# A new hand-written order of steps, six weight staging tiles and one PSUM pool in a fused RWKV and squared-ReLU kernel

## Chip, cores and metric

The kernel runs on one core of a Trainium2 chip. The metric is device time in microseconds (us); the kernel before takes 173.77 us (median of 3 runs, 173.72 to 174.05). One core has five engines with queues of their own: TensorE (PE, with its weight loads PEld), VectorE (DVE), ScalarE (ACT), GpSimd (POOL) and SyncE (SP, which here only issues DMAs). A wait on one engine holds all that stands behind it in that engine's queue.

## What is computed

```python
# attention: B, H, S, D = 4, 8, 768, 48
for t in range(S):
    cur = einsum('bhd,bhe->bhde', u * k[t], v[t])
    y[t] = einsum('bhd,bhde->bhe', r[t], state + cur)
    state = w * state + einsum('bhd,bhe->bhde', k[t], v[t])
# feed-forward: x = y as 3072 tokens of 384; w_in 384 x 2048, w_out 2048 x 384
h = maximum(x @ w_in, 0)
out = (h * h) @ w_out
```

All inputs and the output are float32; the kernel computes its matmuls in bfloat16.

## The kernel before

The sequence is cut into 24 chunks of 128 tokens: chunk i is part i // 4 of batch i % 4. Each chunk goes through the same steps, and each step is a method of the class `Do`. `ld` loads r, k or v of a chunk (192 KB each, on SP). `rh` and `kh` scale r and k by powers of w (L339, L336) into a bfloat16 tile `rk`; `T` transposes that tile with eight matmuls on the identity into a PSUM bank (L363) and `Tc` copies it to SBUF, or `XB` does the same by a transposing DMA (L369). `A` makes the two 128 x 512 products of k and r (L376), and `Bm` masks each half on DVE (L384). `Y` multiplies that by v and, from chunk 4 on, adds the part of the carried state (L392, L394). `P0`, `P1`, `du` and `dv` make the term with u, `xs` adds it to Y (L411). `vb` is v in bfloat16. `U` is this chunk's share of the state (L403); `S0`, `ts` and `S` carry the state on. `X` and `xTc`, or `xX` as a DMA, transpose xs into xT (L429, L436).

The feed-forward works on groups: two of one chunk, then eleven of two (`GROUPS`). `F1.g.s` is a slice s of 512 columns of x @ w_in for group g (L445): twelve matmuls for a group of one chunk, six for a pair. `re` takes the ReLU out of PSUM on ACT or DVE (L453, L455), `sq` squares it (L460, L462, L464) into one of 30 `hq` tiles. `F2.i.q` adds a quarter of the second product for chunk i, four matmuls (L472); `os` copies the sum and `out` stores it. `F2c` is F2 for the last chunk in two column parts (L486). `Z.n.b` is filling: n // 4 matmuls of 512 columns and n % 4 of 128 on the identity, whose result nobody reads (L498, L500).

The first weight goes in eight pieces `W1` of 384 KB in float32: seven by `lW` on SP into a staging tile (four tiles, `wsa`) with a cast `cW`, one (W.0.2) by a DMA that casts, issued by POOL. The second weight goes in four pieces `W2` (W.1.0 to W.1.3) by such DMAs from POOL (L333).

Nothing schedules at run time. The text `ORDER` lists all steps; each engine's queue holds its own in that order, and semaphores make a step wait for what it reads and for the tile that it overwrites. A step reads `what:engine/slots`:

```python
for step in ORDER.split():
    what, how = step.split(":")
    name, *at = what.split(".")
    eng, *given = how.split("/")
```

`F1.2.4:P/0` is slice 4 of group 2 on TensorE into slot 0 of its pool. PSUM has eight banks in three pools: four for the attention steps, two for F1 (`bankH`), two for F2 (`bankO`). F2's four quarters of a chunk come in the order 0 to 3.

Of the kernel before, what the change touches and what calls it, by code (L numbers as in the profile page):

```python
# [40 lines left out]
xTc.4:A P1.7:D XB.7:S/6 F2.2.3:P kh.9:D/2 P0.9:D/3 T.6:P/3 rh.9:D F1.3.4:P/0 ld.k.10:S/2 F2.3.3:P Tc.6:A/0 P0.6:D/2
ld.k.8:S/3 vb.6:A/7 re.3.4:A/0 F1.3.3:P/1 A.6:P/2/1 re.3.3:A/4 ld.r.8:S/1 P1.6:G ld.v.8:S/1 os.3:D/2 A.7:P/0/3
F1.3.1:P/0 du.7:D/1 F1.3.5:P/1 S.5:G Bm.6.0:D/3 kh.8:G/1 U.7:P/2 Bm.6.1:D/1 ld.v.10:S/2 re.3.1:A/3 du.6:D/2 re.3.5:A/2
dv.6:G Bm.7.1:D/2 U.4:P/1 Bm.7.0:D/0 sq.3.3:A0/16 F1.3.0:P/0 F1.3.2:P/1 re.3.0:A/5 sq.3.1:A0/17 Y.6:P/3 dv.7:G Y.7:P/0
ld.v.9:S/3 F1.3.7:P/0 ts.4:D/1 XB.9:S/1 out.3:S re.3.2:A/1 xs.6:D/1 sq.3.0:A0/18 vb.8:A/2 U.6:P/1 os.2:D/3 rh.8:G
kh.10:G/0 X.6:P/3 XB.8:S/3 sq.3.2:A0/19 ld.k.11:S/4 F1.3.6:P/1 F2.5.0:P/1 ld.r.10:S/3 F2.4.0:P/0 xs.7:D/2 X.7:P/0
F2.4.1:P xTc.6:A/2 ld.r.11:S/4 F2.5.1:P ts.7:D/0 re.3.6:A/4 re.3.7:D/3 xTc.7:A F1.4.4:P/1 P0.8:G/4 kh.11:G/6 F1.4.6:P/0
S.4:D ld.r.12:S/5 ld.k.13:S/5 sq.3.7:A0/20 ts.6:D/1 P1.8:D sq.3.4:A0/21 du.8:D/3 ld.r.13:S/6 sq.3.5:A0/22 S.7:D
re.4.4:A/5 A.9:P/3/2 sq.3.6:A0/23 dv.8:G ld.v.11:S/5 re.4.6:A/1 A.8:P/0/1 P1.9:D Bm.8.1:D/4 F1.4.1:P/1 rh.10:G P0.11:G/0
F2.4.2:P Bm.8.0:D/5 XB.10:S/2 vb.9:A/1 F1.4.2:P/0 re.4.1:A/3 Bm.9.0:D/3 Y.8:P/1 Bm.9.1:D/1 U.8:P/0 du.9:D/4 ld.k.14:S/6  # L50
F1.4.3:P/1 P1.11:G xs.8:D/3 sq.4.1:A0/24 re.4.2:A/0 sq.4.2:A0/25 F1.4.0:P/0 dv.9:G sq.4.4:A0/26 U.9:P/3 re.4.0:A/2
rh.11:D F2.4.3:P re.4.3:A/4 sq.4.0:A0/27 os.4:A/2 Y.9:P/2 F1.4.7:P/0 X.8:P/1 XB.11:S/4 sq.4.3:A0/28 xs.9:D/4 F1.4.5:P/1
xTc.8:A/0 ts.8:D/0 F2.6.0:P/0 ld.k.15:S/1 X.9:P/2 P0.13:D/1 rh.13:G/4 F2.5.2:P re.4.7:D/3 P0.10:D/2 re.4.5:A/0 xTc.9:A
ld.r.15:S/0 S.6:D vb.10:A/3 sq.4.7:A0/29 F2.6.1:P S.8:G F1.5.7:P/0 out.4:S F1.5.5:P/1 re.5.7:A/5 F2.5.3:P du.11:D/0
F1.5.1:P/0 ts.9:D/1 P1.10:G A.11:P/1/0 Bm.11.0:D/0 sq.4.5:A0/1 vb.11:A/0 A.10:P/2/3 re.5.5:A/2 F1.5.0:P/1 kh.13:G
sq.5.5:A0/0 F2.6.2:P Bm.11.1:D/2 re.5.1:A/4 Bm.10.1:D/5 F1.5.4:P/0 os.5:A/2 U.11:P/1 du.10:D/2 re.5.0:A/3 U.10:P/0
# [61 lines left out]
def kernel(  # L118
# [443 lines left out]
```

## Time and profile before

| what | value |
|---|---|
| device time, median of 3 runs (lowest to highest) | 173.77 us (173.72 to 174.05) |
| span of the profiled execution, first to last instruction | 172.5 us |
| median time minus that span | 1.27 us |
| busy time of PE, DVE, ACT, POOL | 161.6, 130.3, 111.1, 80.8 us |
| DMA | 29.13 MB, mean 169 GB/s |

The profile of one execution numbers every time from the start of its span. "[1.41 <-DVE rk L336]" behind an instruction is the idle time of its engine before it and what ended it. In a row of the timeline stand start, length, engine, line, operation and tiles (written <- read), merged to a count; a matmul's modelled end includes the pipeline, so that rows overlap. In the view by stretches each engine has its busy time and, in brackets, its instructions; at the end stand the granted TensorE clock, the share of DMA time and GB/s. In the chain of waits each row is a piece of the path that ended last: start, length, and what it was.

### The profile page before, as it was taken

To read this page: it belongs to the slowest core of one execution; us is meant where nothing else is said; L and a number is where in the kernel's file an instruction comes from. 1 tells how busy PE (TensorE), PEld (TensorE's weight loads), DVE (VectorE), ACT (ScalarE), POOL (GpSimd) and SP (SyncE) were. 2 spreads that over 40 slices of the span, in tenths; PEclk is the share of its full clock that TensorE was granted. 3 is DMA by queue.
4 is the path that set the end of the run, shared out by engine and by line. 5 is a ranking of instruction groups with operands and counts; after the bars stand their busy time and mean duration, and the time that the engine had idled before them with its cause. 6 is when DMAs were issued, how large, how long until landed. Compare 5 with 4: busy or idle time off the path is not lost.

```text
span 172.5 us, 4388 instructions
## 1 busy us (share of the span) xinstructions
PE 161.6 (94%) x1702; PEld 121.2 (70%) x1702; DVE 130.3 (76%) x259; ACT 111.1 (64%) x207; POOL 80.8 (47%) x98
## 2 busy tenths in 40 slices
PE   3976799979999999999999999999999999999992
PEld 1444788745788787787778768777778778777671
DVE  5768977739999896598789889888889894538300
ACT  2358787746379899858649647848858726532430
POOL 5644895108659298966937364047660204000000
PEclk9999999999999999999999999999999999999999
DMA  5999899989999989979999997998988330331022
GB/s 99 223 244 306 227 188 207 195 166 200 204 212 184 202 177 214 241 174 184 204 189 215 177 229 153 180 181 186 154 217 159 85 114 4 87 141 48 23 78 84
DMA packets 105588, 29.13 MB, mean 169 GB/s; under 512 B 98008, under 2 KB 105568, under 8 KB 105568
## 3 DMA queue, kind: packets, MB, share of 16 engines
q1 hardware_dynamic: 103672, 26.95, 72.7%
q0 software_dynamic: 1744, 1.77, 6.1%
q8 instruction: 13, 0.21, 0.5%
q10 hardware_dynamic: 152, 0.14, 0.2%
q14 instruction: 7, 0.06, 0.1%
HBM read 20.46 MB, written 4.72 MB: 146 GB/s over the span
## 4 chain that ended last, share of the span: by engine, by line
PE 76%; DMA 12%; SPq 8%; ACT 1%; POOL 1%; issue 1%; DVE 0%; POOLq 0%
PE bank L472 33%; PE bank L445 31%; DMA ldk<-in_k_dram 8%; SPq L320 6%; DMA wsa<-in_moe_w_in_dram 4%; PE bank L376 3%; PE bank L394 2%; PE bank L392 2%; SPq L324 2%; PE bank L403 2%; PE bank L486 2%; PE bank L429 1%; PE bank L363 1%; ACT W L260 1%; POOL urow L218 0%
## 5 line engine op out<-in xcount | busy, mean ns | idle before, releaser
L445 PE MATMUL bank<-xT,W 128*128 128x256 bf16 (+1 forms) x624 | 74.9, 264 | 0.2
L472 PE MATMUL bank<-W,hq 128*128 128x384 bf16 x368 | 69.3, 326 | 0.0
L453 ACT ACTIVATE hr<-bank 128x512 bf16<-128x512 f32 x75 | 44.4, 596 | 32.6 <-PE bank L445 27.1
L445 PEld LDWEIGHTS <-W 128*128 128x128 bf16 x624 | 55.2, 98 | 10.6 <-DVE hr L455 0.3
L472 PEld LDWEIGHTS <-hq 128*128 128x128 bf16 x368 | 34.8, 98 | 17.6
L460 ACT ACTIVATE hq<-hr 128x512 bf16<-128x512 bf16 x65 | 39.1, 628 | 0.3
L384 DVE TENSOR_TENSOR Bm<-bank,maskJT 128x512 bf16<-128x512 f32 x48 | 31.3, 684 | 7.3 <-PE bank L376 7.2
L346 POOL TENSOR_TENSOR P<-P,ub 128x384 f32<-128x384 f32 x15 | 16.1, 1079 | 13.9 <-DVE P L342 13.6
L455 DVE TENSOR_SCALAR hr<-bank 128x512 bf16<-128x512 f32 x21 | 14.3, 687 | 8.5 <-ACT hq L460 3.8
L342 POOL TENSOR_TENSOR P<-ldr,ldk 128x384 f32<-128x384 f32 x14 | 14.3, 1022 | 9.6 <-DMA ldk<-in_k_dram 6.0
L336 POOL TENSOR_TENSOR rk<-ldk,Wkhat 128x384 bf16<-128x384 f32 x10 | 10.0, 996 | 16.9 <-DMA ldk<-in_k_dram 16.9
L411 DVE TENSOR_TENSOR xs<-bank,dv 128x384 bf16<-128x384 f32 x24 | 13.0, 552 | 5.0 <-POOL dv L354 2.8
L354 POOL TENSOR_TENSOR dv<-ldv,du 128x384 f32<-128x384 f32 x18 | 14.8, 829 | 0.0
L349 DVE TENSOR_REDUCE du<-P 128x8 f32<-128x384 f32 x24 | 13.0, 544 | 0.6 <-POOL P L346 0.4
L260 ACT COPY rkT<-bank 128x1024 bf16<-128x1024 bf16 x7 | 7.1, 1012 | 9.1 <-PE bank L363 9.1
L339 POOL TENSOR_TENSOR rk<-ldr,Wt 128x384 bf16<-128x384 f32 x9 | 9.0, 996 | 7.0 <-DMA ldr<-in_r_dram 7.0
L260 ACT CAST vb<-ldv 128x384 bf16<-128x384 f32 x19 | 9.6, 511 | 4.1 <-DMA ldv<-in_v_dram 4.1
L498 PE MATMUL bank<-identity 128*128 128x512 bf16 x29 | 9.5, 471 | 2.7 <-POOL identity masks.py:199 2.7
L260 ACT COPY os<-bank 128x384 f32<-128x384 f32 (+1 forms) x15 | 7.0, 469 | 6.8 <-PE bank L472 4.5
L262 DVE COPY os<-bank 128x384 f32<-128x384 f32 (+1 forms) x10 | 5.2, 524 | 7.9 <-PE bank L486 4.3
L394 PE MATMUL bank<-vb,Bm 128*128 128x48 bf16 x192 | 11.0, 183 | 0.0
L464 DVE TENSOR_TENSOR hq<-hr 128x512 bf16<-128x512 bf16 x27 | 10.9, 432 | 0.0
(66 smaller groups left out, 166.5 us busy)
## 6 DMA issues: line engine op xcount, KB each, us to landing
ldk<-in_k_dram SPq DMA_DIRECT2D x24, 192.0 KB, 3.6
ldr<-in_r_dram SPq DMA_DIRECT2D x24, 192.0 KB, 3.6
ldv<-in_v_dram SPq DMA_DIRECT2D x24, 192.0 KB, 4.0
out_dram<-os SPq DMA_DIRECT2D x23, 192.0 KB, 2.3
wsa<-in_moe_w_in_dram SPq DMA_DIRECT2D x7, 384.0 KB, 5.6
W<-in_moe_w_out_dram POOLq DMA_DIRECT2D x4, 384.0 KB, 9.9
rkT<-rk SPq DMA_TRANSPOSE x17, 3.5
W<-in_moe_w_in_dram POOLq DMA_DIRECT2D x1, 192.0 KB, 6.3
```

The lines of the kernel that those rows point to most:

```text
L260: e.copy(o, a)
L342: e.tensor_mul(P0b[slot[f"P{i}"]], loaded("r", i), loaded("k", i))
L346: e.tensor_mul(t, t, ub)
L349: e.tensor_reduce(dub[slot[f"dv{i}"]], P0b[slot[f"P{i}"]], axis=mybir.AxisListType.X, op=ALU.add)
L354: e.tensor_mul(dvb[slot[f"dv{i}"]], loaded("v", i), t)
L384: e.tensor_mul(Bmb[slot[f"Bm{i}{h}"]], heads(bank(f"bA{i}{h}"), 128), mask_b)
L394: e.matmul(y[:, hc, D * h : D * (h + 1)], m[h][:, hc, :], vb[:, 2 * hc + h, :], start=(c == 0), stop=True, skip_group_check=True,)
L445: e.matmul(hp[:, fi, :], W1[f // 2][:, c, 128 * (f % 2) : 128 * (f % 2 + 1)], xt[:, c, :], start=(c == 0), stop=(c == CCH - 1), skip_group ...
L453: e.activation(hr, hp, AF.Relu)
L455: e.tensor_scalar_max(hr, hp, 0.0)
L460: e.activation(hq, hr, AF.Square)
L472: e.matmul(bank(f"bO{i}", "bO")[:, 0:d_model], hqb[slot[f"hq{g},{f // m}"]][:, at : at + L], W2[q][:, f % 4, :], start=(f == 0), stop=(f = ...
```

## The change

The whole of `ORDER` is new. The steps are the same ones, apart from Z; their order on every engine, the engine of some of them and their slots are drawn anew by a model that plays the engines in time order. Counted by engine: on DVE re 21 to 31, xTc 0 to 6, vb 1 to 4, cW 0 to 1, S 10 to 5, kh 14 to 10, P0 10 to 8, P1 9 to 6, os 10 to 8, sq 31 to 25; on ACT re 75 to 65, sq 65 to 71, vb 19 to 9, xTc 14 to 8, os 15 to 17; on POOL S 6 to 11, kh 10 to 14, P0 14 to 16, P1 15 to 18, vb 4 to 11, cW 3 to 2. Z goes from 17 steps (29 matmuls of 512 columns, 7 of 128) to 6 (38 and 14).

The four staging tiles become six (`st`), and the three PSUM pools one of eight banks, where any step can have any bank. F2 names its first f-block and a count, so that the quarters of a chunk may come in any order:

```diff
-POOLS = dict(ldr=7, ldk=7, ldv=7, ws=0, wsa=4, rk=7, P0=5, dv=5, vb=8, rkT=7, bank=4, bankH=2, bankO=2, Bm=6, xs=5, xT1=2, xT2=3, xT4=1, hr=6, hq=30, os=4, ts=2)
+POOLS = dict(ldr=7, ldk=7, ldv=7, st=6, rk=7, P0=5, dv=5, vb=8, rkT=7, Bm=6, xs=5, hr=6, hq=30, os=4, ts=2, xT1=2, xT2=3)
...
-    def bank(var, kind="b"):
-        return banks[first[kind] + slot[var]]
+    def bank(var):
+        return banks[slot[var]]
...
-        def F2(e, i, q):
+        def F2(e, i, f0, nf):
...
-            for f in range(4 * q, 4 * q + 4):
+            for f in range(f0, f0 + nf):
                 at = L * n * (f % m) + L * j
+                summed[i] += 1
                 e.matmul(
-                    bank(f"bO{i}", "bO")[:, 0:d_model],
+                    bank(f"bO{i}")[:, 0:d_model],
                     hqb[slot[f"hq{g},{f // m}"]][:, at : at + L],
-                    W2[q][:, f % 4, :],
-                    start=(f == 0), stop=(f == FCH - 1), skip_group_check=True,
+                    W2[f // 4][:, f % 4, :],
+                    start=(summed[i] == 1), stop=(summed[i] == FCH), skip_group_check=True,
```

The other edits add forms that this version does not use (`PAIRED = 0`, `WIDE = False`, `WCP = False`) and rename tiles (`Wk` to `WkQ`). So the queues begin as follows. SP before, then after:

```
ld.k.1 ld.r.1 u ld.r.3 ld.r.0 ld.k.0 ld.v.1 ld.k.3 ld.r.2 ld.v.0 ld.k.2 lW.0.1 lW.0.6 ld.v.2 lW.0.7 lW.0.0 ld.v.3 lW.0.5 lW.0.4 wc lW.0.3 ld.r.4 ld.k.4 ld.r.5 ld.k.5 ld.k.7 ld.v.5 ld.v.4 ld.r.7 ld.r.6 ld.k.6 ld.v.7
ld.r.0 ld.k.3 u ld.k.0 ld.r.3 ld.r.1 ld.r.2 ld.k.2 ld.k.1 lW.0.0 ld.v.0 lW.0.1 ld.v.3 ld.v.1 ld.v.2 lW.0.4 lW.0.5 lW.0.6 lW.0.7 lW.0.3 ld.r.4 wc ld.k.4 ld.r.5 ld.k.5 ld.r.7 ld.k.7 ld.v.4 ld.v.5 ld.k.6 ld.r.6 ld.v.7
```

TensorE after (slots left out; F2.i.f.4 is four f-blocks from f):

```
Z.83 T.3 T.0 Z.31 A.0 A.3 T.1 Z.22 A.1 T.2 U.0 Y.0 Z.15 X.0 A.2 Z.8 Y.3 Y.1 U.3 F1.0.0 X.3 U.2 X.1 Y.2 F1.1.0 Z.7 F1.0.2 F1.1.2 F1.1.3 X.2 F1.0.3 F1.2.4 F1.2.1 F1.2.3 F1.2.7 F1.2.5 F1.1.1 U.1 F1.2.0 F1.2.6 F1.2.2 F1.0.1 F2.1.0.4 F2.2.0.4 F2.3.0.4 F2.0.0.4 T.4 F2.2.4.4 F2.3.4.4 T.5 F2.0.4.4 F2.1.8.4 A.5 A.4 F2.1.4.4 F2.2.8.4 F2.2.12.4 F2.0.8.4 F2.0.12.4 U.4 Y.4 F2.3.12.4 Y.5 F2.1.12.4 X.4 U.5 X.5 F2.3.8.4 T.6 F1.3.3
```

TensorE before, from the first F1 on:

```
F1.1.3 Y.2 X.0 F1.1.0 F1.0.0 Y.3 X.2 U.0 F1.0.3 X.3 U.3 F1.0.2 F1.1.2 F1.2.1 F1.2.4 F1.2.5 U.1 F1.2.7 F1.0.1 F1.1.1 F1.2.3 F2.0.0 F1.2.2 F2.1.0 F1.2.6 F1.2.0 F2.1.1 F2.0.1 T.4 F2.0.2 F2.1.2 A.4 T.5 F2.0.3 F2.1.3 A.5 F2.3.0 F2.2.0 F2.2.1 Y.4 U.5 Y.5 F2.2.2 F2.3.1 X.4 X.5 F2.3.2 F2.2.3 T.6 F1.3.4 F2.3.3
```

POOL after: `P0.0 P0.3 P1.3 P1.0 P0.1 P1.1 vb.0 dv.0 vb.3 dv.3 dv.1 vb.2 P0.2 P1.2 cW.0.5 W.0.2 cW.0.3 W.1.0 W.1.1 WLm kh.4 P1.4 W.1.2 W.1.3 rh.7 kh.7`. ACT after, from the first copy: `Tc.3 Tc.0 Tc.1 cW.0.0 cW.0.1 Tc.2 vb.1 xTc.0 xTc.3 cW.0.4`. DVE after, from xTc.1: `xTc.1 re.0.0 du.2 dv.2 cW.0.7 xs.2 xTc.2 re.0.2 sq.0.2 sq.1.3 rh.4 re.2.1 sq.2.1 P0.4 sq.1.2 S0.2 S0.1`.

More of the change, by code (lines that the diff above doesn't have):

```diff
@@ L52 @@
[L52 to L56, printed above, removed]
@@ L240 @@
+    nc.gpsimd.memset(maskP if PAIRED else maskJT, 1.0)
+    if PAIRED:
+        for p in rows:
+            above(nc.gpsimd, maskP[p, :], L // 2 + 1)
+    else:
+        above(nc.gpsimd, maskJT, L)
     mask_b = bass.AP(
@@ L371, in A @@
         def A(e, i):
+            if i < PAIRED:
+                tk, tr = [rkTb[slot[f"rkT{x}P{i // 2}"]].rearrange("q (j c) t -> q j c t", j=2) for x in "kr"]
+                for hc in range(HP):
+                    for h in range(2):
+                        q = slice(64 * h, 64 * h + D)
+                        for p in rows:
+                            e.matmul(
+                                heads(bank(f"bA{i}{h}"), 128)[p, hc, :].rearrange("p (j t) -> p j t", j=2),
+                                tk[q, i % 2, hc, p],
+                                tr[q, :, hc, p],
+                                start=True, stop=True, skip_group_check=True,
+                            )
+                return
             t = rkTb[slot[f"rkT{i}"]]
```

463 lines of the change are left out of this document (301 added, 162 removed).

## The prediction

> **What bounds the kernel now.** I read the page first, then the busy times by stretch, then the chain of waits in order of time, then the timeline of the first 48 us.
>
> ```profile
> span 172.5 us, 4388 instructions
> ...
> PE 161.6 (94%) x1702; PEld 121.2 (70%) x1702; DVE 130.3 (76%) x259; ACT 111.1 (64%) x207; POOL 80.8 (47%) x98
> ...
> PE   3976799979999999999999999999999999999992
> ...
> DMA  5999899989999989979999997998988330331022
> ```
>
> ```profile
> 25.00:48.00 23.00, 21.44 (x225) 15.79 (x223) 17.91 (x36) 13.85 (x26) 10.31 (x13) 1.00 1.08 195
> 48.00:160.00 112.00, 112.00 (x1186) 86.20 (x1184) 92.43 (x176) 78.09 (x151) 54.38 (x57) 1.00 0.78 165
> ```
>
> The second row (PE is the first busy figure) decides the frame: from 48 to 160 us TensorE is never idle, so there only its amount of work counts. Between 25 and 48 us it is idle for 23.00 - 21.44 = 1.56 us. Before 25 us much of its time goes to Z, the filling matmuls on the identity. The DMA digits are 9 for the first two thirds.
>
> ```profile
> 24.58 13.90 DMA ldk<-in_k_dram
> 38.50 0.57 DVE rk L336
> 39.12 0.62 PE bank L363 x8
> ...
> 166.68 2.65 PE bank L486 x32
> 169.33 0.02 issue
> 169.35 0.37 ACT os L260
> ```
>
> The one long wait of the dense part: the load k5 lands 13.9 us after its issue, kh.5 follows, and T.5 starts only at 39.12. At the end nothing but F2c, one copy and its store are left: 172.5 - 169.33 = 3.2 us, and the new order ends the same way, with the last copy on DVE instead of ACT.
>
> All times below are of this execution, span 172.5 us. The median of the runs, 173.77, lies 1.27 us above the span; I add 1.27 at the end.
>
> **The change part by part.** Counted from the two orders, TensorE does the same work but for Z: 96 F1, 92 F2, 2 F2c, 24 A, 24 Y, 20 U, 14 X and 7 T in both; Z goes from 29 wide and 7 narrow matmuls to 38 and 14. So three things count: how late the dense work starts, what waits stand in it, and whether the new order brings waits after 48 us.
>
> *Start, to 25.4 us.*
>
> ```profile
> 2.70 5.18 PE L498 MATMUL bank<-identity 128*128 128x512 bf16 x13 [2.70 <-POOL identity masks.py:199]
> ...
> 3.53 0.15 PEld L498 LDWEIGHTS <-identity 128*128 128x128 bf16 x1 [0.28 <-issue]
> 3.96 0.15 PEld L498 LDWEIGHTS <-identity 128*128 128x128 bf16 x1 [0.28 <-issue]
> ...
> 8.91 1.01 ACT L260 COPY rkT<-bank 128x1024 bf16<-128x1024 bf16 x1 [2.89 <-PE bank L363]
> ...
> 14.49 1.28 DVE L384 TENSOR_TENSOR Bm<-bank,maskJT 128x512 bf16<-128x512 f32 x2
> ...
> 15.09 1.24 PE L498 MATMUL bank<-identity 128*128 128x512 bf16 x5
> ...
> 16.75 0.56 DVE L411 TENSOR_TENSOR xs<-bank,dv 128x384 bf16<-128x384 f32 x1 [0.52 <-ACT rkT L260]
> ...
> 17.05 0.89 ACT L260 CAST W<-wsa 128x768 bf16<-128x768 f32 x1
> ...
> 17.85 0.48 ACT L260 COPY xT<-bank 128x384 bf16<-128x384 bf16 x1
> ...
> 20.59 1.56 PE L445 MATMUL bank<-xT,W 128*128 128x128 bf16 x24
> ...
> 25.66 1.21 PEld L445 LDWEIGHTS <-W 128*128 128x128 bf16 x12 [0.29 <-DVE hr L455]
> ```
>
> A wide Z first takes 0.43 us (3.53 to 3.96), later (1.24 - 0.17 of pipeline) / 5 = 0.21; 13 in 5.18 us means ten slow ones. Z.83 (20 wide, 3 narrow) thus lasts 4.3 + 2.1 + 0.2 = 6.6 us, to 9.3, though T.3's inputs are there at about 7.4. T.3 and T.0 follow, their copies Tc.3 and Tc.0 (1.01, spaced 0.92) end at 12.0 with Z.31 beside them, and A.0 starts at 12.0 (before: 11.45). Two Bm (0.60 apart) end at 13.75; T.1, Z.22, A.1, T.2 and U.0 keep TensorE until 15.2; then Y.0, xs.0 (0.56, with Z.15 beside it), X.0 at 16.3, and on ACT Tc.2, vb.1, xTc.0 until 17.6. A.2, Z.8, Y.3, Y.1 and U.3 stand ahead of F1.0.0, which starts at 18.3. F1.1.0, F1.0.2 and F1.1.2 follow (0.76 each) behind X.3, X.1, Y.2 and two casts (0.89), to 22.85.
>
> ```profile
> 7.75 1.00 POOL L342 TENSOR_TENSOR P<-ldr,ldk 128x384 f32<-128x384 f32 x1 [0.72 <-DMA ldk<-in_k_dram]
> ...
> 9.42 1.00 POOL L342 TENSOR_TENSOR P<-ldr,ldk 128x384 f32<-128x384 f32 x1 [0.67 <-DMA ldk<-in_k_dram]
> ...
> 19.17 0.90 ACT L260 CAST W<-wsa 128x768 bf16<-128x768 f32 x1 [0.84 <-DMA wsa<-in_moe_w_in_dram]
> ```
>
> Next comes the data. The fifth load of 192 KB is there at 7.7, the seventh at 9.4; twelve units of 192 KB later (a W1 piece is two) the piece W1.0 is there at 19.15: 0.81 us a unit. In the new SP order W1.7 ends the 24th unit: 7.7 + 19 x 0.81 = 23.1, its cast on DVE (no such row; between 0.6 and 0.9, I take 0.65) ends at 23.75, and F1.1.3 waits 0.9 us for it. The six staging tiles remove SP's waits for a cast; since DMA is full all the same, the bytes come no sooner, and I cost them at nothing (at best the 0.9). F1.1.3, X.2 and F1.0.3 end at 25.4. The old order has done exactly this set when it starts F1.2.1 at 25.66. So this stretch is worth 0.25 us; bounds: -1.0 (W1.7 a us later) to +1.0 (W1.7 on time).
>
> *25.4 us to the point where groups 0 to 2 are through F2 and T.6 is done.*
>
> ```profile
> 47.56 0.82 PE L445 MATMUL bank<-xT,W 128*128 128x256 bf16 x6
> 48.21 0.81 PE L472 MATMUL bank<-W,hq 128*128 128x384 bf16 x4
> ```
>
> F1 is spaced 0.65 and F2 likewise; the smaller ones come from their spacing in the chain. The rest of this set is 8 F1 of group 2 (5.2), two short F1 (1.5), 16 F2 (10.4), three T (1.35), two each of A, Y, U, X (2.0) and U.1: 20.6 us. Before, it ends at 47.56 + one F2 + one U = 48.4, so 22.7 us with 2.1 of waits, T.5's 1.6 the largest. The new order puts T.5 behind as much useful work (21.0 us against 21.2), but the loads r5 and k5 now have fewer weight loads beside them: W.1.2 and W.1.3 stand on POOL behind kh.4, which needs k4.
>
> ```profile
> 24.23 2.18 POOL L333 DMA_DIRECT2D W<-in_moe_w_out_dram  x3
> ```
>
> ```profile
> W<-in_moe_w_out_dram POOLq DMA_DIRECT2D x4, 384.0 KB, 9.9
> ```
>
> The first row issues W.1.1 to W.1.3; the second is the page's, with the median from issue to landing last. In the 13.9 us from k5's issue to its landing, DMA moved nearly all four W2 pieces and four loads of 0.81: at most (13.9 - 3.2) / 4 = 2.7 us for a piece; I take 2.4, since the end of W.0.2 is in it. By the same bytes in the new order, with two pieces still to come and a little of them under way, k5 lands at about 34.8 (an estimate). kh.5 ends at 35.5 to 36.5, T.5 is due at 36.7: no wait. Instead W.1.2 and W.1.3, issued at about 31 and 32, are due at 37.8 (F2.1.8) and 40.2 (F2.2.12). I put their landing at 37 and 39, so no wait, with little cover. On DVE rh.4 and P0.4 wait for r4 and k4 with re.2.1 and S0.2 behind them, whose banks F1.1.1 (28.7) and F1.2.2 (30.9) need: a cover of some 0.4 us. ACT's Tc.5 before A.5 is even (38.35 against 38.45). TensorE then reaches the point at 46.0 to 46.1: 2.3 us sooner than before.
>
> *After it.* The same work at the same spacing; a gain or a loss can only be new waits. Lead of the data: A stands about 2 us of TensorE work later in the new order for most chunks, SP's loads are in nearly the same order, so the lead after the 2.3 us is about as before. Banks: with one pool of eight the shortest TensorE work between an old holder's last write and the next one's first, after the start, rises from 0.9 to 1.07 us. What shrinks is F1 to F2: the TensorE work between an F2 and the last F1 that it needs. Its least was 2.6 us; now 22 of 92 have under 2.5 and 13 under 2.0, the least 1.64.
>
> ```profile
> 30.37 0.60 ACT L453 ACTIVATE hr<-bank 128x512 bf16<-128x512 f32 x1 [0.17 <-PE bank L445]
> 31.00 0.63 ACT L460 ACTIVATE hq<-hr 128x512 bf16<-128x512 bf16 x1
> ```
>
> Those rows give what it needs with ACT free: pipeline end 0.17 (0.82 - 0.65), then 30.33 to 31.63 = 1.30, and a start: 1.5 us. With every one of them 0.3 us late, the sum of what lies over is 0.57 us (seven F2); I charge 0.5. Bounds: nothing, and the price of the third rival.
>
> *Engines.* DVE gives five S, four kh, two P0 and three P1 to POOL, ACT gives ten re and six xTc to DVE and most vb to POOL. ACT and DVE come out lighter or level; POOL gains about 14 operations of 1.0 and seven casts, some 18 us on its 80.8: still idle over a third. I cost that at nothing; the cover is the lead of the chunks, and what it costs without it is the third rival.
>
> Sum: 172.5 - 0.25 - 2.05 + 0.5 = 170.7; with 0.3 for the even places of the first 46 us, 171.0. With 1.27: **172.3 us**.
>
> **Rivals.**
>
> *The W2 pieces come late.* If W.1.2 takes the median 9.9 us from its issue at 31.0, it lands at 40.9; F2.1.8 stands at the head of TensorE's queue from 37.8, with everything behind it: 3.1 us lost, span 174.1, time 175.4, slower. It decides from a landing later than about 39.3, where the gain is used up. For: k4, which holds POOL ahead of W.1.2, may itself come late. Against: the 9.9 holds a queue of four pieces issued within four us of each other; the new order issues them in two pairs.
>
> *Nothing is left.* W1.7 half a us late and a wait of a us at W.1.2 or T.5 take the 1.5: about 173.8, no difference. For: every step of the second stretch is due within about a us of its data.
>
> *F1 to F2 misses.*
>
> ```profile
> 55.93 1.00 POOL L342 TENSOR_TENSOR P<-ldr,ldk 128x384 f32<-128x384 f32 x1
> ...
> 56.24 1.10 DVE L424 TENSOR_TENSOR S0W<-ts,WLm 128x384 bf16<-128x384 f32 x1
> ...
> 57.92 0.55 DVE L346 TENSOR_TENSOR P<-P,ub 128x384 f32<-128x384 f32 x1
> ...
> 76.67 0.55 DVE L336 TENSOR_TENSOR rk<-ldk,Wkhat 128x384 bf16<-128x384 f32 x1
> 76.83 1.25 POOL L346 TENSOR_TENSOR P<-P,ub 128x384 f32<-128x384 f32 x1 [1.34 <-DVE P L342]
> ```
>
> A DVE operation of two SBUF operands that began beside a POOL one took 1.10 us, its like 0.55 alone; where POOL began second, POOL took 1.25 and DVE its 0.55. With more of POOL such lateness is more frequent. If each close F2 is late by one such 0.55, 13 of them wait, 3.0 us in sum: span 173.5, time 174.8, slower. It decides from about 0.45 us of common lateness. Against it: most of the close ones run re and sq on ACT, idle for 34 of 112 us from 48 on, and the operations that leave DVE are the very kind that stretches. The Trainium skill, GPSIMD Engine Reference, section 8, Key points, says that GpSimd shares its SBUF interfaces with VectorE and contends with DVE instructions that have two SBUF inputs. By that, such operations on either engine would stretch wherever they meet; the trace agrees (1.10, 1.25), and shows that the later one pays.
>
> **How the numbers follow.** Forecast 172.3: chance 0.54. W2 late, 175.4: 0.18. Nothing left, 173.8: 0.13. F1 to F2 misses, 174.8: 0.15. Lowest: both bounds good (1.0 at the start, no late places): 172.5 - 1.0 - 2.05 + 1.27 = 170.7; I leave a little of that out. Range 171.0 to 175.6, the forecast's own 171.2 to 173.4. A measurement here can tell about 0.2%, 0.35 us, from no change. Faster by more: 0.56 (the forecast but for its upper edge, and a little of the second rival); within: 0.14; slower: 0.30.
>
> **What would show it.** Right: T.3 at about 9.3 and the first F1 at about 18.3; F1.1.3 held by the cast of W1.7; T.5 without a wait on kh.5; the first F1 of group 3 at about 46 instead of 47.56; TensorE without idle time afterwards. Wrong: a wait of F2 on W2, idle TensorE time before F2 ended by ACT's or DVE's hq after 50 us, or a first F1 after 19.1.

## The result and the profile after

The new kernel takes 175.59 us (median of four runs, 175.45 to 175.81), the old one in the same comparison 173.75 (four runs, 172.99 to 174.05): ratio 1.0121, 95% interval 1.0087 to 1.0155. It is slower by 1.2%; I had forecast 172.3, faster. The result lies in the range, at its upper edge, on the other side. Ratios here and below leave out runs that lie more than 1.5% above the fastest of their kernel.

The page of the new kernel, profiled in a run of 175.66 us; the digits are busy tenths in 40 slices:

```profile
span 173.5 us, 4403 instructions
...
PE 163.4 (94%) x1718; PEld 121.8 (70%) x1718; DVE 138.6 (80%) x257; ACT 105.8 (61%) x189; POOL 100.3 (58%) x118
...
PE   3999989989999999999997999899999999998992
...
DMA  4999999999998989999799893994991451321202
...
PE 57%; DMA 13%; DVE 8%; SPq 8%; POOL 6%; issue 3%; ACT 2%; DVEq 0%; POOLq 0%
...
L594 PE MATMUL bank<-xT,W 128*128 128x256 bf16 (+1 forms) x624 | 71.0, 264 | 2.0 <-DMA xT<-xs 1.3
L622 PE MATMUL bank<-W,hq 128*128 128x384 bf16 x368 | 68.4, 326 | 0.2 <-ACT hq L609 0.2
```

The last two rows are F1 and F2: of the 2.0 us that TensorE idled ahead of F1, 1.3 were ended by the transposes xX; ahead of F2 it hardly idled.

The busy times of the same stretches as before the change (the first figure after the length is TensorE's):

```profile
25.00:48.00 23.00, 22.41 (x235) 16.88 (x233) 21.22 (x39) 16.70 (x32) 10.37 (x14) 1.00 1.13 201
48.00:160.00 112.00, 109.49 (x1148) 82.69 (x1147) 94.06 (x166) 69.26 (x127) 72.64 (x76) 1.00 0.78 160
```

From 25 to 48 us TensorE idles 0.6 us instead of 1.6. From 48 to 160, where it never idled, it now idles 2.5 us. TensorE's rows in order of time show where the first stretches stand and where the idle time lies (in brackets: idle before the row, and what ended it):

```profile
8.86 1.06 PE L464 MATMUL bank<-identity,rk 128*128 128x128 bf16 x16
...
17.66 0.83 PE L594 MATMUL bank<-xT,W 128*128 128x128 bf16 x12
...
23.34 0.51 PE L594 MATMUL bank<-xT,W 128*128 128x128 bf16 x6 [0.69 <-DVE W L288]
...
36.57 0.62 PE L464 MATMUL bank<-identity,rk 128*128 128x128 bf16 x8 [0.59 <-DVE rk L428]
...
46.05 1.69 PE L594 MATMUL bank<-xT,W 128*128 128x256 bf16 x14
...
92.67 0.40 PE L494 MATMUL bank<-rkT 48*128 48x128 bf16 x8 [1.05 <-DMA rkT<-rk]
...
109.08 1.16 PE L594 MATMUL bank<-xT,W 128*128 128x256 bf16 x9 [0.61 <-DMA xT<-xs]
...
159.67 1.58 PE L594 MATMUL bank<-xT,W 128*128 128x256 bf16 x13 [0.64 <-DMA xT<-xs]
```

The first five rows are the forecast's points: T.3 and T.0 at 8.9, the first F1 at 17.7, F1.1.3 held by the cast of W1.7, T.5 with a short wait only, the first F1 of group 3 at 46.05. The last three are new: A.14 waits for XB.14, F1.8.0 for xX.14, F1.12.1 for xX.22. Counted by the spacing of steps, beyond the usual spacing of their kind, they cost 1.22, 0.78 and 0.81 us; F2.15.8 adds 0.35. From 46.05 to the end of TensorE's last instruction (170.31) the new kernel takes 124.3 us; the old one takes 120.9 from the same point (48.4) to 169.32. So 2.35 us are won by 46 us and 3.3 lost after it. That holds for these two executions: their spans differ by 1.0 us, the times by 1.84, so that 0.8 us of the loss are placed by neither figure.

The chain of waits into the second of these, then SP's queue (issue times) ahead of the first:

```profile
98.67 3.17 DMA ldv<-in_v_dram
...
101.89 0.51 POOL vb L288
102.40 0.79 POOL dv L449
103.19 1.28 POOL P L441
...
104.97 0.55 DVE xs L560
105.54 3.49 DMA xT<-xs
```

```profile
81.99 3.20 SPq L388 DMA_DIRECT2D ldr<-in_r_dram  x2
85.29 1.33 SPq L474 DMA_TRANSPOSE rkT<-rk  x1
86.67 1.26 SPq L388 DMA_DIRECT2D ldk<-in_k_dram  x2
88.04 1.62 SPq L474 DMA_TRANSPOSE rkT<-rk  x1
```

v14, which F1.8.0 needs through vb, dv, xs and xX, is issued at 98.67 only. XB.14 (the last row of SP's) is issued behind XB.15 and two loads, and SP's rows follow each other without a gap: from 74 to 92 us it issues 19 entries and never stands still for over 0.15 us. So the place in this queue is a time. Places (first entry 1) and issue times in us, old and new:

```
          old          new                 old          new
ld.k.14   54th  65.57  66th  75.69   ld.k.19    96.90  77.63
XB.14     69th  80.57  79th  88.04   ld.r.19    98.89  81.99
ld.v.14   71st  83.62  88th  98.67   ld.k.21   113.83  87.30
xX.12     76th  88.41  84th  93.09   ld.v.16    95.27  80.60
```

What chunk 14 needs stands 4 (r14) to 17 entries further back; loads for chunks 16 to 21 stand ahead of it. F1.12.1's wait is of another kind: between 125 and 160 us DMA is busy for only 0.43 of the time.

The engines in the stretch before the first wait, old and then new:

```profile
48.00:75.00 27.00, 27.00 (x314) 21.58 (x312) 22.36 (x42) 24.04 (x47) 21.36 (x23) 1.00 1.01 209
```

```profile
48.00:75.00 27.00, 27.00 (x296) 20.67 (x295) 23.93 (x43) 18.70 (x35) 25.70 (x27) 1.00 1.00 193
```

DVE, ACT and POOL are the third to fifth busy figures. GpSimd is busy for 25.7 of 27 us, and ScalarE has become the idle one; DMA (the last but one figure) is full in both.

### The profile page after: what moved, and what is told of

It is laid out like the page before. It is cut to its first block, busy times and chain, and to the rows that moved or that the text cites. A ratio compares the mean times of both kernels' runs of the same rounds, so it can differ in the third digit from the quotient of the medians.

```text
span 173.5 us, 4403 instructions
## 1 busy us (share of the span) xinstructions
PE 163.4 (94%) x1718; PEld 121.8 (70%) x1718; DVE 138.6 (80%) x257; ACT 105.8 (61%) x189; POOL 100.3 (58%) x118
## 4 chain that ended last, share of the span: by engine, by line
PE 57%; DMA 13%; DVE 8%; SPq 8%; POOL 6%; issue 3%; ACT 2%; DVEq 0%; POOLq 0%
PE bank L594 25%; PE bank L622 23%; SPq L388 6%; DMA xT<-xs 5%; DMA st<-in_moe_w_in_dram 4%; DMA rkT<-rk 3%; DVE hq L613 2%; PE bank L494 2%; SPq L399 2%; DMA ldv<-in_v_dram 2%; PE bank L531 2%; PE bank L636 2%; PE bank L527 1%; ACT hr L602 1%; ACT hq L609 1%
## 5 line engine op out<-in xcount | busy, mean ns | idle before, releaser
L594 PE MATMUL bank<-xT,W 128*128 128x256 bf16 (+1 forms) x624 | 71.0, 264 | 2.0 <-DMA xT<-xs 1.3
L602 ACT ACTIVATE hr<-bank 128x512 bf16<-128x512 f32 x65 | 38.1, 592 | 24.6 <-PE bank L594 22.5
L609 ACT ACTIVATE hq<-hr 128x512 bf16<-128x512 bf16 x71 | 43.3, 627 | 13.5 <-DVE hr L604 12.3
L604 DVE TENSOR_SCALAR hr<-bank 128x512 bf16<-128x512 f32 x31 | 21.1, 685 | 10.4 <-PE bank L594 10.1
L449 POOL TENSOR_TENSOR dv<-ldv,du 128x384 f32<-128x384 f32 x18 | 16.4, 913 | 14.2 <-DVE du L444 9.4
L441 POOL TENSOR_TENSOR P<-P,ub 128x384 f32<-128x384 f32 x18 | 18.9, 1055 | 7.0 <-DVE P L437 6.4
L437 POOL TENSOR_TENSOR P<-ldr,ldk 128x384 f32<-128x384 f32 x16 | 16.6, 1042 | 3.4 <-DMA ldk<-in_k_dram 3.4
L573 POOL TENSOR_TENSOR S0W<-ts,WLm 128x384 bf16<-128x384 f32 x11 | 11.1, 1017 | 9.5 <-DVE ts L570 9.3
L428 POOL TENSOR_TENSOR rk<-ldk,Wkhat 128x384 bf16<-128x384 f32 x14 | 15.3, 1097 | 2.2 <-DMA ldk<-in_k_dram 2.1
L286 ACT COPY os<-bank 128x384 f32<-128x384 f32 (+1 forms) x17 | 7.9, 462 | 13.4 <-PE bank L622 11.5
L531 PEld LDWEIGHTS <-Bm 128*128 128x128 bf16 x192 | 9.3, 96 | 1.3 <-DVE Bm L507 0.7
```

What stands on the lines that cost most here:

```text
L428: e.tensor_mul(scaled("k", i), loaded("k", i), early("WkQ") if i < EARLY else Wkhat)
L437: e.tensor_mul(P0b[slot[f"P{i}"]], loaded("r", i), loaded("k", i))
L441: e.tensor_mul(t, t, ub)
L449: e.tensor_mul(dvb[slot[f"dv{i}"]], loaded("v", i), t)
L531: e.matmul(y[:, hc, D * h : D * (h + 1)], m[h][:, hc, :], vb[:, 2 * hc + h, :], start=(i < B), stop=True, skip_group_check=True,)
L594: e.matmul(hp[:, fi, :], W1[f // 2][:, c, 128 * (f % 2) : 128 * (f % 2 + 1)], xt[:, c, :], start=(c == 0), stop=(c == CCH - 1), skip_group ...
```

## The experiments

The runs below scatter more: those of the old kernel spread from 173.5 to 178.8 us. Kernels are therefore compared by their ratio to runs of the old kernel on the same chip, and traces by where TensorE waits. Theories: **Places** (or Lead): a few waits, each set by a place in a queue. **Engines**: GpSimd and VectorE are short of time. **Loads**, later **Queue**: the sequence on SP. **Closeness**: F2 too near its F1 (my third rival). **Shortage** (also called Lead in some expectations): the chunks' data as a whole comes no sooner, so a wait removed comes back elsewhere.

The waits of TensorE after 48 us in the kernels that keep the new order, in us (spacing beyond the usual; those over 0.3 in the last column):

```
          A.14 F1.7.6 F1.8.0 F1.12.1  others
new       1.22   -     0.78   0.81    F2.15.8 .35
h2_new    0.16  1.66   0.92   0.82    -
e1_xb14    -    0.21   1.28   0.80    F1.9.1 .31
e2_v14    1.43  0.31    -     0.74    F2.10.0 .74
e3_xs22   1.55  0.72   1.05   0.80    F2.10.0 .32
e4_all     -    0.78   0.60   0.79    F2.12.12 .92, F1.9.1 .52, F2.13.4 .36, F2.15.8 .31
f2_loads  1.39  0.33   0.49   0.83    -
g3_pool    -    0.28   1.39   0.82    F1.5.0 1.41, F2.15.8 .51, F1.7.1 .34
g4_tiles  1.41  0.35   0.56   0.80    F1.9.1 .78, F2.10.0 .74
j1_out18  1.37  0.36   1.40    -      F2.10.0 .30
```

### One wait at a time

e1_xb14: `XB.15:S/6 +XB.14:S/0 ld.k.16:S/2 ... ld.k.21:S/5 ... -XB.14:S/0 A.14:P/3/5`

> One step moved: the transpose XB.14 is issued directly behind XB.15, ahead of the loads k16 and k21. Theory Lead (what is lost after 46 us are a few waits for transfers of chunks 14 and 22, each set by a place in a queue): XB.14 is issued at about 86.7 instead of 88.0 and lands at about 90.7, A.14 no longer waits (1.22 us), but chunk 14 has a second wait at F1.8.0 (0.78), whose chain does not move, so that this one can grow by up to the 1.2: span 172.3 to 173.5, time 174.4 to 175.6. Rival Engines (VectorE and GpSimd carry more than they can between 75 and 110 us, a cured wait comes back elsewhere): time 175.6. Rival Closeness (F2 waits for hq everywhere): A.14 was an accident, time 174.4.

Ratio 1.0042 (0.9996 to 1.0089). A.14 follows A.15 without a gap, and F1.8.0 waits longer:

```profile
92.33 0.62 PE L491 MATMUL bank<-rkT 48*128 48x128 bf16 x16
```

```profile
109.80 0.39 PE L591 MATMUL bank<-xT,W 128*128 128x256 bf16 x2 [1.11 <-DMA xT<-xs]
```

x16 in the first row is A.15 and A.14 in one. TensorE came earlier to a step whose data had not moved: part of the gain only changes its place, as the first theory had allowed for. Two places on SP were enough for A.14: XB.14 lands at 90.16, and at 93.95 in e3, which has the unchanged order up to there.

e2_v14: `xX.12:S/2 +ld.v.14:S/3 XB.16:S/2` and `+xs.14:D/0 du.16:D/1`

> Two steps moved: the load v14 ahead of XB.16 on SP's queue (issue at about 94.4 instead of 98.7), and xs.14 ahead of du.16 on VectorE. Theory Lead: xs.14 ends at about 104.2 instead of 105.5, xX.14 is issued 1.3 us sooner, and F1.8.0 does not wait (0.78): span 172.7, time 174.8. Rival Engines: GpSimd's vb.14 and dv.14 stay late behind S.12 and vb.16, time 175.4 or more. Rival Closeness: 174.8 too.

Ratio 1.0025 (0.9978 to 1.0072). F1.8.0's wait is gone: xX.14 lands at 109.74, and at 111.36 in e3, where F1.8.0 waits 1.05 us after as much waiting ahead of it. A.14's wait stays, and one of 0.74 stands before F2.10.0: its bank is read by Bm.12.0, which stands behind the cast of v17 on VectorE, and VectorE idled 2.67 us for that load.

e3_xs22: `sq.11.3:D2/18 +xs.22:D/4 ... sq.11.7:D2/26 -xs.22:D/4`

> One step moved: xs.22 goes ahead of four squares on VectorE, directly behind sq.11.3. Theory Lead: xs.22 ends at about 154.1 instead of 155.0, xX.22 is issued behind xX.23 at about 154.5 and lands before 158.9, F1.12.1 does not wait (0.81): span 172.7, time 174.8. Rival Engines: the squares behind it are 0.55 us later and F2.20.8 or F2.20.12 waits instead: 175.3. Rival Closeness: F2.20.8 waits, 175.3 as well.

Ratio 1.0101 (1.0040 to 1.0162). A miss for all of them: F1.12.1 waits 0.80 as before, and no F2 behind the edit waits instead. (xs.22 passes three squares, sq.11.4, 11.5 and 11.7, and not four.)

e4_all: the edits of e1, e2 and e3 together.

> The moves of the three kernels before it together. Theory Lead: all three waits go, 2.8 us in sum: span 170.7, time 172.8, faster than the old kernel by 0.5%. Rival Engines: other waits take their place, the sum is under 1.0 us: time 174.6 or more. Rival Closeness: what stays after the three waits is over 1.0 us of small waits ahead of F2; time about 173.5.

Ratio 1.0037 (0.9987 to 1.0088). A.14's wait is gone and F1.8.0's is not, and new ones stand at F1.7.6, F2.12.12 and F1.9.1: over 4 us in sum. F1.7.6 and F1.9.1 wait for transposes xX, but F2.12.12 and F2.13.4 for banks that VectorE's xs.15 and Bm.16.1 empty late. The 2.8 us did not come. By its ratio up to two thirds of the loss may be recovered, though the profiled run (177.47 us) is 0.9 us above the median of the runs compared; the intervals of e1, e2 and e4 don't settle that against the 1.0045 to 1.0162 of h2_new.

j1_out18: the edit of e3, and `-out.18:S ... xX.22:S/1 +out.18:S`

> e3_xs22 and, besides, the store out.18 behind xX.22 on SP. Theory Places: xX.22 is issued about 0.6 us sooner relative to TensorE, and F1.12.1 waits 0.2 us instead of 0.80; nothing else changes, ratio as the new order's less 0.003: 1.005 to 1.012. Rival Shortage (xX.22 waits for VectorE's squares or for DMA): the wait stays at 0.6 to 0.8.

Ratio 1.0007 (0.9955 to 1.0059). TensorE's rows at F1.12.1, in e3 and in j1:

```profile
161.73 0.49 PE L591 MATMUL bank<-xT,W 128*128 128x256 bf16 x3 [0.64 <-DMA xT<-xs]
```

```profile
161.58 1.58 PE L591 MATMUL bank<-xT,W 128*128 128x256 bf16 x13
```

The wait is gone. xX.22 stood behind squares on VectorE and behind a store on SP; moving xs.22 alone showed nothing, and moving the store alone was not tried.

### One part of the change undone

f1_engines: from F1.3.3 on, for example `-kh.14:G/0 +kh.14:D/0`, `-re.7.1:D/3 +re.7.1:A/3`, `-P1.12:D +P1.12:G`; 119 steps.

> The new order, but from F1.3.3 (46 us) on every step runs on the engine that it had in the old kernel: 119 steps change engine, none its place. Ratios are to the old kernel, the new one being 1.012. Theory Engines (GpSimd, with some 18 us more, and VectorE hold the chunks up between 75 and 110 us while ScalarE idles): most of the 3 us of waits after 46 us go, ratio 0.988 to 0.998. Rival Loads (the new sequence of SP's loads brings k14, v14 and r14 up to 15 us later than the old one, behind loads of chunks 16 to 21): the waits for chunk 14 stay, ratio 1.006 to 1.015. Rival Lead (DMA is full until 110 us, so TensorE's 2.3 us at 46 us must be given back whatever the order): ratio about 1.00 to 1.005.

Ratio 1.0864 (1.0795 to 1.0933): all expectations missed by far. GpSimd is back at 81.4 us busy, and TensorE waits at about 20 steps. A place in the order holds only for the engine that it was drawn for, so this run can't tell the theories apart.

f2_loads: the 48 loads from F1.3.3 on in the old sequence, for example `-ld.k.19:S/4 +ld.v.14:S/2`.

> The new order, but from F1.3.3 on SP's 48 loads go in the old kernel's sequence, at the same places of the order as far as the consumers allow; k14, v14 and r14 stand ahead of v16, v17, k19, r19 and k21 again. Theory Loads: the waits at A.14 and F1.8.0 (2.0 us) go, F1.12.1's 0.8 stays: ratio 0.998 to 1.003. Theory Engines: GpSimd and VectorE stay as late, ratio 1.008 to 1.015. Rival Lead: about 1.00 to 1.005.

Ratio 1.0106 (1.0036 to 1.0176). v14 is issued at 82.1 and k14 at 68.2, near the old kernel's 83.6 and 65.6, and F1.8.0 waits less (0.49); A.14 still waits 1.39. The edit permuted the loads among themselves, so that XB.14 is still the 79th entry on SP and is issued at 89.19. The loads' sequence alone does not do it; that of the transposes among them was not tried here.

f3_both: f1 and f2 together.

> The two kernels before it together: from F1.3.3 on the old engines and the old sequence of loads, but the new order's places of TensorE's steps. Theories Engines and Loads each expect what their own kernel gives, and if both hold the ratio is about 0.988. Rival Closeness (F2 stands too close behind its F1): some 1 us of small waits ahead of F2 stays, 0.995. Rival Lead: 1.00 to 1.005.

Ratio 1.0887 (1.0816 to 1.0959), for f1's reason.

g3_pool: `-S.8:G +S.8:D`, likewise S.9 and S.10; `-vb.13:D/4 +vb.13:A/4`, likewise os.7, xTc.10 and vb.17.

> The new order with GpSimd relieved in the stretch ahead of A.14: S.8, S.9 and S.10 go from GpSimd to VectorE, and vb.13, os.7, xTc.10 and vb.17 from VectorE to ScalarE, which idles 8 us of the 25 there; no step changes place. Theory Engines (GpSimd holds rh.15, kh.14 and with them XB.15 and XB.14 up): rh.15 ends 2 us sooner, XB.14 is issued 1 to 2 us sooner, A.14 does not wait (1.2 us) and F1.8.0 less: ratio 1.000 to 1.006. Rival Queue (SP's queue alone sets XB.14): ratio 1.010 to 1.015 as the new order's.

Ratio 1.0102 (1.0031 to 1.0173). GpSimd's rh.15 and kh.14, and SP's queue, in g3:

```profile
79.14 1.32 POOL L431 TENSOR_TENSOR rk<-ldr,Wt 128x384 bf16<-128x384 f32 x1
80.42 1.31 POOL L425 TENSOR_TENSOR rk<-ldk,Wkhat 128x384 bf16<-128x384 f32 x1
```

```profile
85.37 1.41 SPq L471 DMA_TRANSPOSE rkT<-rk  x1
...
88.29 1.89 SPq L471 DMA_TRANSPOSE rkT<-rk  x1
```

The unchanged kernel in h2_new (below) has on GpSimd and on SP:

```profile
83.10 1.31 POOL L434 TENSOR_TENSOR rk<-ldr,Wt 128x384 bf16<-128x384 f32 x1
84.37 1.11 POOL L428 TENSOR_TENSOR rk<-ldk,Wkhat 128x384 bf16<-128x384 f32 x1
```

```profile
88.29 2.06 SPq L474 DMA_TRANSPOSE rkT<-rk  x1
```

rh.15 and kh.14 are 4 us sooner, and XB.14 is issued at the same 88.29: its place on SP sets it, and GpSimd does not. Engines falls for this wait. That A.14 does not wait in g3 has another reason: TensorE comes later, since F1.5.0 waits for the bank that os.7, now on ScalarE, empties:

```profile
80.83 0.82 PE L591 MATMUL bank<-xT,W 128*128 128x256 bf16 x6 [1.25 <-ACT os L283]
```

g4_tiles: `POOLS st=6` to `st=4`, and `lW.0.6:S/0 lW.0.7:S/1 lW.0.3:S/2`.

> The new order with four W1 staging tiles instead of six, the pieces taking them in turn. My prediction costed the two more tiles at nothing, since DMA is full all the same: first F1 and F1.1.3 at the same times within 0.3 us, ratio as the new order's, 1.010 to 1.015. Rival: SP waits for a cast ahead of W1.6, W1.7 and W1.3 with r4 and k4 behind them, F1.1.3 is held 0.5 to 1.5 us longer: ratio 1.014 to 1.021.

Ratio 1.0128 (1.0061 to 1.0196), not to be told from h2_new's: the six tiles are worth nothing that shows. F1.1.2 idles 0.80 us in g4's trace for a cast and 0.94 in h2_new's, and the first F1 of group 3 starts at 46.92 and 46.95.

### The old order behind 46 us

f4_hybrid: the new order's steps up to F1.3.3; then all others as the old order has them, `F1.3.4:P/1 ... F1.3.3:P/6 A.6:P/2/7 ...`.

> The new order up to F1.3.3 (46 us), then all steps that are left in the old kernel's order and on its engines, with slots drawn anew (the least recently freed one). Theories Engines, Loads and Closeness all expect that the 2.3 us won by then are kept: ratio 0.987 to 0.990. Rival Lead (the loads come no sooner, so TensorE waits for them later on): TensorE idles 1 to 2.5 us between 48 and 110 us, ratio 0.995 to 1.003.

Ratio 0.9968 (0.9926 to 1.0009). TensorE waits 2.2 us between 49 and 72 us and not at all from 73 to 160. VectorE at the seam:

```profile
47.46 0.55 DVE L425 TENSOR_TENSOR rk<-ldk,Wkhat 128x384 bf16<-128x384 f32 x1
47.93 1.19 DVE L434 TENSOR_TENSOR P<-ldr,ldk 128x384 f32<-128x384 f32 x1
49.04 0.55 DVE L431 TENSOR_TENSOR rk<-ldr,Wt 128x384 bf16<-128x384 f32 x1
49.51 0.55 DVE L434 TENSOR_TENSOR P<-ldr,ldk 128x384 f32<-128x384 f32 x1
49.98 1.28 DVE L504 TENSOR_TENSOR Bm<-bank,maskJT 128x512 bf16<-128x512 f32 x2
```

A.6 is through at 48.2, but its Bm start at 49.98, behind kh.9, P0.9, rh.9 and P0.6; F1.3.0 needs the bank that Bm reads and waits. TensorE is ahead, VectorE is not.

g1_banks: the banks and small buffers drawn again by the times of f4's trace, for example `-F1.3.0:P/2 +F1.3.0:P/0`.

> The hybrid f4 (new order up to F1.3.3, the old one behind it) with its PSUM banks and small buffers drawn again: each step takes the one whose last reader ended earliest in the trace of f4, not the one last read in the order. TensorE's waits of f4 between 49 and 72 us (0.87 before F1.3.0, 0.55 before F1.3.7, 0.78 before F1.5.0) stood at writes into a bank that a late Bm still read. Theory Banks (those waits are the choice of the bank): they go, the 2.3 us won by 46 us are kept, ratio to the old kernel 0.985 to 0.990. Theory Lead (the loads come no sooner, so TensorE has to wait for the chunks' data until it is as late as it was): other waits of 1 to 2 us take their place, ratio 0.995 to 1.000.

Ratio 0.9999 (0.9957 to 1.0040). F1.3.0's wait is gone, and Y.7 waits 0.99 us for the same late Bm: Banks falls.

g2_banks_dve: g1, and `-P0.9 -rh.9 ... Bm.7.0:D/5 +rh.9:D/0 +P0.9:D/3`.

> As g1, and rh.9 and P0.9 go behind the four Bm of chunks 6 and 7 on VectorE, so that Bm.6 does not stand behind work for chunk 9. Theory Banks: nothing more to win, as g1. Theory Lead split by engine: if VectorE's work for chunks ahead holds the Bm up, this takes another 0.3 to 0.8 us off; if the loads do, XB.9 and A.9 come later and nothing is won.

Ratio 1.0010 (0.9957 to 1.0062). Y.7 waits only 0.23 us, but ts.4 and xs.6 now stand behind P0.9, and X.6 waits 1.34.

h1_old and h2_new: the two kernels unchanged.

> The old kernel unchanged, for its spans and its stretches on the chip of this call. Theory Order (all of the loss stands behind 46 us): as in the first profile, no waits of TensorE after 48 us, and about the same time outside the span as h2_new. Rival Outside (part of the loss lies outside the span): time less span is 0.5 to 0.9 us smaller here than in h2_new. Ratio 1.000 by both.

> The new kernel unchanged, on the same chip. Theory Order: the point where groups 0 to 2 are through is reached 1.5 to 2.5 us sooner than in h1_old, and TensorE loses 2.5 to 4 us more than in h1_old from there to the end, in waits at A.14, F1.8.0, F1.12.1 and ahead of F2: ratio 1.008 to 1.014. Rival Head (on the slower chip the first 46 us win nothing): the point comes within 0.5 us of h1_old's.

Ratios 0.9985 (0.9943 to 1.0027) and 1.0103 (1.0045 to 1.0162): the second confirms the first result. The pairs of time and span of the profiled runs are 178.54 and 176.5 for the old kernel, 176.93 and 174.9 for the new one: 2.04 and 2.03 us outside the span, and 1.90 and 2.06 in the mean of all their runs. The rival Outside falls. h1_old's profile is of a run 2.6 us above its median; TensorE waits 1.25 us at F1.7.7 and 0.95 at F1.10.6 there, where no waits were expected, and its stretches are not compared. So the rival Head is not settled by this pair.

h2_new's longest wait stands at F1.7.6; TensorE's row and, ahead of it, two of ScalarE's:

```profile
97.88 0.51 ACT L286 CAST vb<-ldv 128x384 bf16<-128x384 f32 x1 [1.61 <-DMA ldv<-in_v_dram]
98.30 0.47 ACT L286 COPY xT<-bank 128x384 bf16<-128x384 bf16 x1
```

```profile
98.93 0.81 PE L594 MATMUL bank<-xT,W 128*128 128x256 bf16 x6 [1.50 <-DVE ts L570]
```

TensorE's row names ts on VectorE, but F1.7.6 neither reads what ts writes nor overwrites the bank that ts reads: in e4 it starts at 97.56, before those two ts (98.25 and 99.40). What it reads is xT, and its two halves came late through DMA: xX.12, issued at 93.63, landed at 98.79 (5.2 us, 3.7 in the first profile), and xTc.13 (the second row) stood behind the cast of v15, which ScalarE had waited for.

h3_seam: `-rh.9:D +rh.9:G/0`, likewise kh.9 and P0.9; `du.7:D/0 +P0.6:D/2`; `Bm.6.1:D/1 +Bm.7.1:D/3 +Bm.7.0:D/5`.

> The hybrid f4 with banks by time as in g1 (other buffers as in f4), rh.9, kh.9 and P0.9 on GpSimd instead of VectorE, and P0.6 and the four Bm of chunks 6 and 7 ahead of what VectorE did for later chunks. Theory Vector (at 46 us TensorE is 2.3 us ahead, but VectorE is not, and its backlog is what gives the gain back): Bm.7.0 ends 1.5 to 2 us sooner, the waits at F1.3.0, Y.7 and F1.3.7 go, ratio 0.984 to 0.992. Rival Lead (the loads give it back): new waits of over a us between 55 and 80 us, ratio 0.996 to 1.002.

Ratio 0.9958 (0.9909 to 1.0007). The waits at F1.3.0, Y.7 and F1.3.7 are gone, as Vector expects, though Bm.7.0 ends 1.3 us sooner and not 1.5; X.6 (0.85) and A.7 (0.39) wait instead.

i1_keep: h3_seam with `+XB.7:S/1 ld.v.6:S/0`, `+P1.6:G P0.9:G/3`, `Bm.7.0:D/5 +du.6:D/2 +dv.6:G kh.8:G/3`, banks drawn again. i2_banks: the same with h3's banks.

> h3_seam with XB.7 ahead of v6 on SP, P1.6 ahead of P0.9 and dv.6 ahead of kh.8 on GpSimd, du.6 directly behind Bm.7.0; banks drawn anew by time. Places: the two waits (1.24 us) go, waste after 60 us as in h3_seam less 1.2, span about 171, ratio 0.986 to 0.992, faster than both kernels. Shortage: another wait of about a us comes before 80 us, ratio 0.994 to 1.000.

> The same steps moved as in i1_keep, with the banks of h3_seam kept. Places and Shortage expect the same as of i1_keep; a difference of over 0.5 us between the two would be the choice of banks.

i1_keep: ratio 0.9931 (0.9895 to 0.9968), faster than both kernels; i2_banks: 0.9996 (0.9953 to 1.0039). The same stretch in f4, h3 and i1, one row from each:

```profile
48.00:75.00 27.00, 25.29 (x295) 20.19 (x290) 21.53 (x40) 23.07 (x46) 20.94 (x22) 1.00 0.98 201
```

```profile
48.00:75.00 27.00, 26.09 (x309) 20.84 (x309) 21.46 (x40) 23.43 (x47) 22.19 (x23) 1.00 0.98 201
```

```profile
48.00:75.00 27.00, 26.49 (x312) 21.10 (x309) 22.22 (x39) 23.14 (x47) 22.55 (x23) 1.00 0.93 187
```

TensorE's idle time goes from 1.7 to 0.9 to 0.5 us, by steps moved to where another queue idled. Some comes back (0.67 at Y.11, 0.86 at F1.8.7), less than was won. i2's trace, where TensorE reaches F1.2.4 0.8 us later than in i1's, waits 1.08 at F2.6.0 for a bank whose reader xs.9 is late; whether the banks make the whole difference is not shown.

## Why the prediction was wrong

*Start, to 25.4 us*: right in its steps. T.3 at 8.9 (9.3 forecast), first F1 at 17.7 (18.3), F1.1.3 held by the cast of W1.7 (0.69; 0.9 forecast), set done at 24.7 (25.4): worth 1.0 us and not 0.25. The cast took 0.95 and not 0.65. The tiles at nothing: right (g4).

*25.4 us to the end of groups 0 to 2*: worth 1.35 us and not 2.05. T.5, which was to start without a wait, waited 0.59 for kh.5. That the sum came out, 46.05 against 46.0 to 46.1, is luck: two misses of 0.7 cancel, and in the other profiles of the table above the first F1 of group 3 starts at 46.2 to 47.4. The first rival, late W2 pieces, did not come.

*After it*: this is the step that failed, at the sentence "SP's loads are in nearly the same order, so the lead after the 2.3 us is about as before". It looked at loads, and not at the whole of SP's queue with its transposes and stores; and what holds for the first loads does not for chunk 14, whose entries stand 4 to 17 places further back. I had the two facts that make a place a time: DMA's digits of 9, and that for the W1 pieces "the bytes come no sooner". I used them for the first 25 us only. With DMA full (busy for 0.99 of the time from 75 to 92 us), loads issued early for chunks 16 to 21 are paid for by those behind them. The sum charged 0.5 us after 46 us and it came to 3.3: 2.8 us more, less the 0.3 for even places that was not needed, is the whole miss of 2.5 in the span (171.0 forecast, 173.5). The lead is not kept by the old order either: in f4 TensorE waits 2.2 us between 49 and 72 us, since VectorE is not ahead.

*Engines*, "I cost that at nothing": no loss could be put down to it at A.14 (g3), but F2.12.12's wait in e4 (0.92) ends with xs.15 on VectorE, which works without a pause from 97.65 to 103.46 there, so that some loss to VectorE's load is not excluded. The mean that I argued from ("still idle over a third") was the wrong figure all the same, 25.7 of 27 us in the stretch that counts, and F1.8.0's chain runs through GpSimd's vb.14, dv.14 and P1.16 (rows above).

What the runs show of the cause: it lies in the order behind 46 us, since the six kernels with the old order there have ratios of 0.9931 to 1.0010, where the new one is at 1.010 to 1.012. Inside it, each of the three waits of the first profile goes when steps on SP are moved: two places for A.14 (e1), v14 ahead of two transposes, with xs.14, for F1.8.0 (e2), a store put behind xX.22, with xs.22, for F1.12.1 (j1). That these waits make the whole loss is not shown: e4 keeps those at F1.8.0 and F1.12.1, and others come up, two of them behind VectorE. And the same kernel waits at other steps in another execution (new and h2_new in the table): 1.66 at F1.7.6, for transfers that landed late from about the same issue times. The three cures with j1's store were not tried together, nor the old sequence of SP's whole queue under the new order, nor the pool of eight banks or F2's free order of quarters by itself; f1 and f3 were to split engines from places and could not.

*Rivals*. "F1 to F2 misses" gave 174.8 and a loss after 46 us of nearly the right size, but for the wrong reason: TensorE's idle time ahead of F2 is 0.2 us in the new profile (second group row), with F2.15.8 as its one wait over 0.3. What was late were the transposes XB and xX, and not hq.

*With 1.27*: this term was mis-sized. The profile's span stood beside a median of other runs. In pairs of time and span from one run, the time outside the span is 1.91 to 2.16 us in the four runs of the new kernel (2.16 in the profiled one) and 1.66 to 2.20, 1.96 in the mean, in 135 runs of the old kernel. By that the old kernel's profile was of a long execution, its typical span about 171.8 (173.75 - 1.96, an estimate). The forecast's 171.0 us with 2.16 would have been 173.2, a gain of 0.3% instead of 0.8%; the term holds 0.9 of the 3.3 us by which the time was missed.

## What to carry to other kernels

Where DMA is full, a DMA queue that never stands still turns the place of an entry into a time: when an order is redrawn, compare the place of every entry, transposes and stores included, with the consumer's place, for the whole run, since the first thirty said nothing of the rest here. A gain ahead of a stretch in which the bounding engine never idles is kept only if what feeds it is as far ahead: compare the others at the same point of its work. A wait mended singly tells what held it, not what it costs: count what the next step then waits.

## What the runs showed of the hardware

Where operations of two SBUF operands on VectorE and GpSimd overlap, the later one takes longer (1.10 and 1.25 us in the prediction's rows), and this can run on from one operation to the next. In h3_seam, where rh.9 and kh.9 moved to GpSimd:

```profile
45.12 1.34 POOL L431 TENSOR_TENSOR rk<-ldr,Wt 128x384 bf16<-128x384 f32 x1 [0.45 <-DMA ldr<-in_r_dram]
...
46.10 0.77 DVE L570 TENSOR_TENSOR S0W<-ts,WLm 128x384 bf16<-128x384 f32 x1
...
46.41 1.32 POOL L425 TENSOR_TENSOR rk<-ldk,Wkhat 128x384 bf16<-128x384 f32 x1
...
46.79 1.35 DVE L438 TENSOR_TENSOR P<-P,ub 128x384 f32<-128x384 f32 x1
```

S.5 begins in rh.9 and ends 0.41 us after it (46.87, 46.46); kh.9 begins in S.5 and ends 0.86 after it (47.73); P1.7 begins in kh.9 and ends 0.41 after it (48.14). Each is the later one of a pair, so that both engines lose: 1.35 instead of 0.55 on VectorE, 1.32 instead of 1.00 on GpSimd. The Trainium skill, SBUF — State Buffer, section "SBUF: two separate sides", calls the shared ports an exclusive lock that the first holds for its whole instruction, while the other blocks; the trace agrees. Work moved between these two engines can therefore cost more than its row where both are busy.

On SP a transposing DMA holds the queue for 1.3 to 2.1 us (XB.15 and XB.14 above), a load for some 0.63 (1.26 for two) and up to 2.2 (3.20 for two, r19 at 1.0 and r16 at 2.15). An entry behind one transpose is issued later by that much.
